# Attention and expert block in one kernel: the first 45 attention steps in another order, 50 of their small jobs on another engine

## The chip, the cores and the metric

The kernel runs on one core of one Trainium2 chip. A core has a matrix engine (TensorE, PE), three engines for the work on vectors (VectorE or DVE, ScalarE or ACT, GpSimd or POOL), a sync engine (SP) that here issues nearly all transfers, and 16 DMA engines. Each engine works through its own queue in the order in which the program was written. The metric is the time of one execution in microseconds (us) on the device. Lower is better.

## The reference

```python
def _attn_ref(q, k, v, tau):                      # (8, 8, 576, 64) each
    scale = 1.0 / np.sqrt(q.shape[-1])
    scores = scale * np.matmul(q, k.transpose(0, 1, 3, 2))
    thresh = np.max(scores, axis=-1, keepdims=True) - tau
    scores = np.where(scores >= thresh, scores, -1000000000.0)
    scores = scores - np.max(scores, axis=-1, keepdims=True)
    attn = np.exp(scores)
    attn = attn / (np.sum(attn, axis=-1, keepdims=True) + 1e-09)
    return np.matmul(attn, v).astype(np.float32)
...
    x = np.ascontiguousarray(attn_out.transpose(0, 2, 1, 3)).reshape(B * S, H * D)   # (4608, 512)
...
    h = x @ w_in                                  # w_in (512, 2048)
    g = np.where(h > 0.0, h, alpha * (np.exp(np.minimum(h, 0.0)) - 1.0))
    return (g @ w_out).astype(np.float32)         # w_out (2048, 512)
```

Attention for 64 heads that keeps only scores within tau of the row's maximum, followed by a two-layer block with an ELU between the layers. All data is float32 when it reaches the engines; the two weight matrices arrive in 64 bits and are converted on the chip.

## The kernel before, in words

Attention works on pairs of heads; there are 32 pairs (8 sequences of 4 pairs). A pair is cut into five **steps**: four blocks of 128 rows for both heads, and one "tail" step for the last 64 rows of both. Step n is `steps[n]`; the steps 10, 13, 16, 19, 24, 29, 34, 39, 44 are tails. Each step is a chain of **jobs** on different engines:

- `sc` (L537, matmuls at L551, PE): scores into one of a few score buffers in PSUM; from step 10 on there are two, so `sc` of a head waits for the mask of the head two before it;
- `max` (L600, DVE), `th` (L604, POOL: maximum minus tau) and `exp` (L614, ACT);
- `mask` (L623, DVE): compares scores with `th`, multiplies with `exp`, and adds up the row; this frees the score buffer;
- `su` and `rec` (sum of the two parts, L631 on DVE or L590 on ACT; reciprocal, L637 on DVE);
- `norm` (L596 on POOL or L584 on ACT): multiplies the row with the reciprocal;
- the result is then transposed, either on PE (`part`, L640, copied out of PSUM by ACT in `put`, L656), or by way of DRAM (`turned`: DVE transposes 32 x 32 squares at L716 and SP writes them out at L745; `fetch`: SP reads them back at L753 or L762, named `landed` in the table of places). The second way is used from step 24 on for most steps;
- `val` (L777 and L782, PE): values times transposed weights, copied out by ACT (`out`, L899).

Mixed in between are: the loading of heads (`load`, SP) and their preparation (`prep`, `scale`, `copy`); the conversion of 32 pieces of the weights, each a load `lw` (L408, SP), `rest` (L415 on ACT or L432 on POOL), `shift` (L421, DVE), `add` (L427, POOL), `sign` (L437, ACT) and `end` (L445, DVE); halves of the two-layer block for the first sequences (`half`: L940 and L980 on PE, with follow-up jobs called `post`); and sums of weight blocks (`in`, L1066, DVE or POOL) that a later stage uses.

The order of all these jobs for the steps 0 to 44 comes from a planner, `early_tasks` (L1135). Each job is entered with a nominal time, to which two numbers of a table `MOVED` are added, one for its kind and one for the job itself:

```python
    def task(x, t, key, f, *needed):
        each = "_".join(map(str, x)) if isinstance(x, tuple) else x
        made[x] = [t + (MOVED.get(key, 0.0) if key else 0.0) + MOVED.get(each, 0.0), len(made), f, needed, False]
...
        for x in sorted(made, key=lambda x: made[x][:2]):
            do(x)
```

`do` first does whatever the job needs and has not been done, and then the job. The result is one sequence of jobs, and each engine's queue is that sequence cut down to its own jobs. The numbers only order; nothing waits for a clock. Four more sets choose engines: `ACT_NORM` (which `norm` jobs are on ACT and not on POOL), `IN_POOL` (which `in` jobs are on POOL and not on DVE), `SU_ACT` (which `su` jobs are on ACT and not on DVE) and `REST_POOL` (which `rest` jobs are on POOL and not on ACT). The number and shape of the jobs do not depend on any of this. What follows step 44, some 1000 us with a fixed interleaving written out by hand (`tail_step`, `wide_step`, `ffn_quarters`), reads a part of the same table under other keys.

Of the kernel before, what the change touches and what calls it, by code (L numbers as in the profile page):

```python
# [18 lines left out]
ACT_NORM = {(0, 1), (10, 0), (10, 1), (11, 1), (13, 0), (15, 1), (16, 0), (17, 0), (17, 1), (18, 1), (22, 0), (24, 0), (25, 0),  # L19
 (26, 1), (28, 0), (30, 1), (31, 0), (32, 0), (33, 0), (35, 0), (36, 0), (36, 1), (37, 0), (40, 1), (44, 0), (44, 1)}  # L20
IN_POOL = {(6, 2), (1, 2), (7, 1), (0, 0), (3, 1), (6, 1), (0, 2), (5, 0), (7, 2), (2, 2), (1, 0), (4, 1), (5, 2)}
SU_ACT = {33, 41, 13, 16, 24, 30}
REST_POOL = {9, 27}

MOVED = {
    "add_10": 0.71, "add_11": -0.15, "add_12": 0.39, "add_14": -0.07, "add_17": 0.55, "add_20": -0.24, "add_21": 0.44,
    "add_22": 5.07, "add_23": -0.73, "add_26": -3.5, "add_27": -0.44, "add_28": -0.38, "add_3": 0.54, "add_30": -0.57,
    "add_31": -0.22, "add_5": 2.32, "add_6": -0.33, "add_8": -0.51, "adda10": 0.84, "adda30": 0.88, "addb00": 0.73,
    "addb01": -4.17, "addb10": -0.32, "addb11": -0.15, "addb20": 0.79, "addb21": 0.43, "addb30": -0.74, "addb31":
    0.02, "adde20": -0.39, "adde21": -0.32, "adde30": -0.22, "adde31": -0.95, "adde40": 0.75, "adde41": 0.21,  # L30
# [12 lines left out]
    "exp0c1": -0.43, "exp0c2": 0.28, "exp0c3": 4.67, "exp0c4": -1.31, "exp0d0": -3.28, "exp0d1": -2.61, "exp0d2":
    -1.48, "exp0d3": -2.62, "exp0d4": -1.52, "exp0e2": 0.41, "exp0e3": 2.22, "exp0z0": 5.23, "exp0z1": 4.88, "exp1a0":
    0.21, "exp1a1": -1.01, "exp1a2": -0.85, "exp1a3": -1.51, "exp1b0": -1.09, "exp1b1": -1.69, "exp1b2": 0.24,
    "exp1b3": -0.46, "exp1c0": 0.46, "exp1c1": 3.31, "exp1c2": 1.51, "exp1c3": 4.64, "exp1d0": -1.25, "exp1d1": 0.19,
    "exp1d2": -2.37, "exp1d3": -3.61, "exp1e2": 0.53, "exp1z0": 0.11, "exp1z1": 1.06, "exp_0_0": 4.58, "exp_0_1":
    -0.35, "exp_11_0": 0.46, "exp_11_1": 2.18, "exp_12_0": 0.57, "exp_12_1": -0.63, "exp_14_0": -0.14, "exp_15_0":
    0.39, "exp_17_0": -0.65, "exp_17_1": 1.88, "exp_18_0": 2.27, "exp_18_1": -0.64, "exp_1_0": 2.83, "exp_20_0":
    -2.39, "exp_22_0": -0.79, "exp_22_1": 1.61, "exp_23_0": 4.02, "exp_24_0": 0.62, "exp_25_0": -0.51, "exp_25_1":  # L50
    -0.17, "exp_26_0": -0.16, "exp_26_1": 0.79, "exp_27_1": -1.13, "exp_28_1": -0.68, "exp_29_0": -0.51, "exp_2_0":
    4.22, "exp_2_1": -0.4, "exp_30_0": 0.01, "exp_30_1": 0.66, "exp_31_1": -0.02, "exp_32_1": -1.23, "exp_33_0":
    -1.92, "exp_34_0": 0.14, "exp_36_1": 0.9, "exp_37_0": 3.69, "exp_37_1": -0.34, "exp_38_0": 0.35, "exp_38_1":
    -3.27, "exp_39_0": -1.11, "exp_3_0": -0.48, "exp_40_0": 3.34, "exp_41_1": -1.16, "exp_42_0": -0.21, "exp_42_1":
    5.99, "exp_43_0": -1.65, "exp_43_1": -0.28, "exp_4_0": 0.68, "exp_4_1": -1.2, "exp_6_0": -0.13, "exp_6_1": -0.48,
    "exp_7_0": -0.49, "exp_7_1": 0.06, "exp_9_0": -0.08, "extra_35": 2.03, "extra_36": -0.7, "extra_37": 0.56,
    "extra_38": -0.08, "extra_39": -0.3, "extra_40": 0.05, "extra_41": -0.31, "extra_42": 1.01, "f0.0": -2.08, "f1.0":
    -0.13, "f1.1": 0.2, "f10.0": 0.05, "f11.0": -0.04, "f12.1": 0.12, "f13.1": -0.5, "f14.0": 0.02, "f15.1": -0.06,
    "f16.0": 0.04, "f16.1": 0.69, "f16.2": -0.14, "f17.0": -0.28, "f18.1": 0.12, "f2.0": -5.54, "f2.1": -0.25, "f2.2":
    0.7, "f20.1": -1.03, "f21.0": 0.13, "f22.1": -0.19, "f23.0": 0.08, "f23.1": 2.72, "f23.2": 0.07, "f25.0": 0.39,  # L60
    "f26.0": -0.08, "f26.1": 0.42, "f3.0": 0.35, "f5.0": -0.32, "f5.1": 4.32, "f6.1": -0.54, "f7.0": -0.01, "f9.0":
    0.35, "f9.1": 1.94, "fbound0": -0.14, "fbound1": 0.93, "fbound4": -0.36, "fe00": 0.1, "fe10": 0.37, "fe11": 0.3,
    "fe20": -0.6, "fetchb0": 0.25, "fetchb1": 0.02, "fetchb2": 2.4, "fetchb3": 0.47, "fetchb4": 0.31, "fetchc0": 0.5,
    "fetchc1": -0.13, "fetchc2": -3.89, "fetchc3": 4.97, "fetchc4": -1.52, "fetchd0": 3.22, "fetchd1": -2.69,
    "fetchd2": 4.68, "fexp00": 0.1, "fexp20": 0.25, "fexp31": 0.12, "ffetch0": 1.19, "ffetch1": -0.24, "ffetch2":
    -0.52, "ffetch3": -0.65, "fkcopy": -0.11, "floadk": -2.59, "floadq": 2.51, "fm00": -3.15, "fm01": -0.49, "fm11":
    -2.07, "fm20": 1.6, "fm21": -0.43, "fmask00": 1.48, "fmask01": -0.63, "fmask10": 0.68, "fmask11": 0.02, "fmask30":
    -0.16, "fmask31": 0.36, "fmask4": 0.2, "fmax00": -0.03, "fmax01": -0.65, "fmax10": 0.91, "fmax11": 0.5, "fmax20":
# [1809 lines left out]
```

## Time and profile before

| what | value |
| --- | --- |
| three runs | 1298.63, 1300.83, 1302.12 us |
| median | 1300.83 us |
| span of the profiled execution, first to last instruction | 1298.8 us |
| mean granted clock of PE | 0.997 |
| busy over the span | PE 1277.1, DVE 1011.8, POOL 790.9, ACT 567.9 us |
| chain that ended last | PE 82%, DVE 4%, DMA 2%, the rest 1% and less each |
| DMA engines | q1 72.1% of their time, 254.14 MB |

The profile is one execution. Busy times of PE are modelled for pipelined matmuls, so that a busy PE is not necessarily PE at its peak; idle times come with the instruction that ended them. The profiled execution's own time was not given apart from its span; the span is 2.0 us less than the median of the three runs and lies within their spread of 3.5 us.

In the steady part of the kernel, from about 320 us on, PE is busy all the time: between 400 and 1000 us its idle time is 0.2 us in sum. The steps 0 to 44 lie in the first 282 us or so.

### The profile page before, as it was taken

How to read it: one execution, taken by the hardware profiler on the slowest of the kernel's cores; microseconds unless marked ns; L12 is line 12 of the kernel's file. 1: busy time of each engine (PE TensorE's matmuls, PEld its weight loads, DVE VectorE, ACT ScalarE, POOL GpSimd, SP SyncE). 2: the span in 40 equal slices, each digit the busy share in tenths (PEclk: the TensorE clock that was granted, in tenths of full speed). 3: DMA queues.
4: the chain of work that ended last, by engine and by line, in shares of the span. 5: the costliest groups of instructions: out<-in, count | busy, mean ns of one | idle time of the engine just before them, and what ended most of it. 6: DMA issues, size and time to landing. Idle time of an engine off the chain costs nothing.

```text
span 1298.8 us, 21747 instructions
## 1 busy us (share of the span) xinstructions
PE 1277.1 (98%) x6822; PEld 993.8 (77%) x6822; DVE 1011.8 (78%) x2199; ACT 567.9 (44%) x1224; POOL 790.9 (61%) x1181
## 2 busy tenths in 40 slices
PE   9999999899999999999999999999999999999998
PEld 7676576446878888878878787878787888888887
DVE  6787887788888988898889889897989882545534
ACT  5888644335262525353444444353525261421320
POOL 4686645767476756766576757574867473524533
PEclk9999999899999999999999999999999999999999
DMA  7546377879898988899889888899899875222211
GB/s 149 129 146 191 97 192 207 250 203 267 210 255 223 269 226 242 236 269 225 237 214 250 240 235 223 254 245 240 227 255 256 229 214 169 89 73 63 92 61 33
DMA packets 327827, 256.01 MB, mean 197 GB/s; under 512 B 209312, under 2 KB 288672, under 8 KB 327712
## 3 DMA queue, kind: packets, MB, share of 16 engines
q1 hardware_dynamic: 325776, 254.14, 72.1%
q8 instruction: 54, 0.88, 0.3%
q10 hardware_dynamic: 1936, 0.48, 0.2%
q14 instruction: 61, 0.50, 0.1%
HBM read 165.94 MB, written 88.60 MB: 196 GB/s over the span
## 4 chain that ended last, share of the span: by engine, by line
PE 82%; DVE 4%; DMA 2%; issue 1%; POOL 1%; ACT 1%; SPq 0%; DVEq 0%; ACTq 0%; POOLq 0%
PE f L1606 30%; PE f L1466 28%; PE sc L829 7%; PE sc L889 7%; PE f L980 3%; PE sc L551 2%; PE f L940 1%; PE sc L881 1%; DMA there<-x 1%; PE pv L782 1%; PE sc L876 1%; DVE x L716 1%; PE rt L640 1%; DVE w L623 1%; DMA sw<-win_sums 1%
## 5 line engine op out<-in xcount | busy, mean ns | idle before, releaser
L596 POOL TENSOR_SCALAR w<-w,rs 128x576 f32<-128x576 f32 x172 | 141.4, 830 | 78.0 <-DVE rs L637 73.3
L836 DVE TENSOR_REDUCE mx<-sc 128x1 f32<-128x576 f32 x207 | 148.2, 749 | 29.6 <-PE sc L829 25.8
L846 ACT ACTIVATE w<-sc,mx 128x576 f32<-128x576 f32 x115 | 82.9, 740 | 117.9 <-DVE mx L836 99.9
L1466 PE MATMUL f<-xt,sw 128*128 128x256 f32 x512 | 123.9, 384 | 1.4 <-ACT xt L899 0.8
L1466 PE MATMUL f<-xt,w_in_sb 128*128 128x256 f32 x512 | 122.3, 381 | 0.1
L842 POOL TENSOR_SCALAR th<-mx,ntau 128x2 f32<-128x2 f32 (+1 forms) x115 | 34.3, 298 | 136.6 <-DVE mx L836 136.6
L716 DVE STREAM_TRANSPOSE x<-w 128x512 f32<-128x512 f32 (+2 forms) x163 | 106.9, 690 | 11.8 <-POOL w L596 10.6
L1466 PEld LDWEIGHTS f<-xt,sw 128*128 128x128 f32 x512 | 93.6, 190 | 21.6 <-issue 4.9
L1466 PEld LDWEIGHTS f<-xt,w_in_sb 128*128 128x128 f32 x512 | 96.2, 190 | 15.9 <-ACT w L1480 2.8
L1466 PE MATMUL f<-x,w_in_sb 128*128 128x256 f32 x448 | 106.1, 379 | 1.3 <-ACT g L1527 1.3
L1606 PE MATMUL f<-w_out_sb,g 128*128 128x256 f32 x448 | 107.1, 382 | 0.0
L1606 PE MATMUL f<-w_out_sb,s 128*128 128x256 f32 x448 | 107.0, 382 | 0.0
L1606 PE MATMUL f<-t,s 128*128 128x256 f32 x448 | 105.8, 379 | 0.0
L829 PE MATMUL sc<-kT,qT 64*128 64x448 f32 (+4 forms) x736 | 103.2, 416 | 0.5 <-DVE w L850 0.5
L829 PEld LDWEIGHTS sc<-kT,qT 64*128 64x128 f32 x736 | 80.6, 186 | 25.5 <-issue 16.8
L1553 POOL TENSOR_TENSOR s<-g 128x256 f32<-128x256 f32 x104 | 80.4, 778 | 29.3 <-PE f L1606 20.0
L850 DVE SCALAR_TENSOR_TENSOR w<-sc,th,w 128x576 f32<-128x576 f32 x115 | 89.7, 810 | 10.2 <-ACT w L846 10.1
L1466 PEld LDWEIGHTS f<-x,w_in_sb 128*128 128x128 f32 x448 | 85.0, 190 | 13.3 <-ACT g L1527 1.7
L1606 PEld LDWEIGHTS f<-w_out_sb,g 128*128 128x128 f32 x448 | 84.1, 190 | 14.2 <-issue 3.2
L1606 PEld LDWEIGHTS f<-w_out_sb,s 128*128 128x128 f32 x448 | 84.2, 190 | 13.5 <-issue 2.5
L1606 PEld LDWEIGHTS f<-t,s 128*128 128x128 f32 x448 | 85.1, 190 | 11.6
L596 POOL TENSOR_SCALAR e<-e,rs 128x576 f32<-128x576 f32 x92 | 68.5, 748 | 35.5 <-DVE rs L637 33.4
(209 smaller groups left out, 2831.5 us busy)
## 6 DMA issues: line engine op xcount, KB each, us to landing
there<-x SPq DMA_DIRECT2D x436, 144.0 KB, 3.6
wTb<-there SPq DMA_DIRECT2D x56, 576.0 KB, 6.5
wTa<-there SPq DMA_DIRECT2D x53, 576.0 KB, 4.9
sw<-win_sums SPq DMA_DIRECT2D x62, 384.0 KB, 4.3
t<-wout_sums SPq DMA_DIRECT2D x45, 512.0 KB, 5.8
qm<-in_q_dram SPq DMA_DIRECT2D x124, 72.0 KB, 4.8
vm<-in_v_dram SPq DMA_DIRECT2D x64, 128.0 KB, 3.7
wst<-in_moe_w_in_dram SPq DMA_DIRECT2D x16, 512.0 KB, 4.4
```

The lines of the kernel that those rows point to most:

```text
L596: nc.gpsimd.tensor_scalar(wv, wv, st["rs"][:, h : h + 1], 1.0, ALU.mult, ALU.mult)
L716: nc.vector.transpose(x[:, :, c0 : c0 + nc_], src.rearrange("p (c g n) -> p g c n", c=nc_, n=T))
L829: on_banks(nc.tensor.matmul(o, qT[r, i * P : (i + 1) * P], kT[r, k0 : k0 + n], start=True, stop=True, skip_group_check=True), o)
L836: on_banks(nc.vector.tensor_reduce(st["mx"][:, h : h + 1], st["sc", h], axis=AX.XY if i == NC else AX.X, op=ALU.max, negate=True), st["sc" ...
L842: nc.gpsimd.tensor_scalar(st["th"][:, cs], st["mx"][:, cs], -1.0, ntau, ALU.mult, ALU.add)
L846: on_banks(nc.scalar.activation(st["e", h], st["sc", h], AF.Exp, bias=st["mx"][:, h : h + 1]), st["sc", h])
L850: on_banks(nc.vector.scalar_tensor_tensor(st["e", h], st["sc", h], st["th"][:, h : h + 1], st["e", h], ALU.is_ge, ALU.mult, accum_out=st[" ...
L889: on_banks(nc.tensor.matmul(o, vm[:, h, c], parts[part][:, g0:g1, h * (NC + 1) + c], start=False, stop=(c == NC - 1), skip_group_check=Tru ...
L980: nc.tensor.matmul(cur[c, i][:, :DM], hidden(c, ft % NU, 1)[:, 0, ft // NU, i], w_out_sb[:, ft], start=(ft == 0), stop=(ft == NFT - 1))
L1466: nc.tensor.matmul(loc["banks"][place], left[:, j], right[:, j], start=(begins and j == 0), stop=(j == 1), skip_group_check=True)
L1553: engine.tensor_tensor(o, x, y, op)
L1606: nc.tensor.matmul(place(m), lhs, rhs, start=(begins and v == 0), stop=(v == RU - 1), skip_group_check=True)
```

## The change

Only constants change; no function does. All four sets change, together in 50 places, and the table `MOVED` gets 356 new entries and new values for 652 of its 1801 old ones; no entry is taken out. All of the changed entries are for single jobs of the steps 0 to 44 (`start`, `rest`, `idle`, `switch` and `late` among them, which are single jobs too). The entries by kind and those of the later stages stay.

```diff
-ACT_NORM = {(0, 1), (10, 0), (10, 1), (11, 1), (13, 0), (15, 1), (16, 0), (17, 0), (17, 1), (18, 1), (22, 0), (24, 0), (25, 0),
- (26, 1), (28, 0), (30, 1), (31, 0), (32, 0), (33, 0), (35, 0), (36, 0), (36, 1), (37, 0), (40, 1), (44, 0), (44, 1)}
-IN_POOL = {(6, 2), (1, 2), (7, 1), (0, 0), (3, 1), (6, 1), (0, 2), (5, 0), (7, 2), (2, 2), (1, 0), (4, 1), (5, 2)}
-SU_ACT = {33, 41, 13, 16, 24, 30}
-REST_POOL = {9, 27}
+ACT_NORM = {(10, 0), (10, 1), (11, 1), (13, 0), (14, 1), (15, 1), (16, 0), (17, 0), (17, 1), (18, 1), (20, 1), (22, 0), (23,
+ 1), (24, 0), (24, 1), (26, 0), (26, 1), (27, 0), (28, 0), (30, 1), (31, 0), (32, 1), (33, 0), (35, 0), (36, 0), (36, 1),
+ (37, 0), (37, 1), (38, 0), (4, 0), (40, 0), (40, 1), (41, 0), (41, 1), (44, 0)}
+IN_POOL = {(1, 0), (2, 2), (3, 2), (4, 0), (4, 1), (4, 2), (5, 2), (6, 1), (6, 2), (7, 1), (7, 2)}
+SU_ACT = {10, 11, 13, 17, 18, 20, 25, 26, 30, 37, 39, 40, 42}
+REST_POOL = {10, 15, 16, 18, 19, 20, 27, 28, 29, 5, 7, 9}
...
-    "mask_15_0": 1.57, "mask_15_1": 1.1, "mask_17_0": 0.6, "mask_17_1": -4.56, "mask_18_0": 5.15, "mask_18_1": -2.03,
...
+    "mask_15_0": -4.95, "mask_15_1": 1.67, "mask_16_0": 0.29, "mask_17_0": 1.53, "mask_17_1": -4.56, "mask_18_0": 3.6,
...
-    5.47, "part_19_0": -0.16, "part_1_2": 0.06, "part_20_0": -0.17, "part_21_1": -0.04, "part_22_1": -3.07,
-    "part_23_1": 2.59, "part_23_2": -0.5, "part_26_0": 0.38, "part_26_1": -0.68, "part_26_2": 0.47, "part_29_0":
...
+    "part_18_1": 0.07, "part_18_2": 7.58, "part_19_0": -1.35, "part_19_1": 0.17, "part_1_2": -0.46, "part_20_0": 5.95,
...
+    0.38, "part_26_1": 2.37, "part_26_2": 0.29, "part_29_0": 0.03, "part_29_1": 1.56, "part_2_0": -2.6, "part_2_2":
```

**The sets.** `ACT_NORM` gains 13 jobs and loses 4 (0,1), (25,0), (32,0), (44,1); `REST_POOL` gains 10; `SU_ACT` gains 11 and loses 4; `IN_POOL` gains 3 and loses 5.

**The order.** Sorting the jobs by the new sums gives, on each queue, a sequence that is close to the old one. On PE, which runs 248 entries of it, ten places differ, each by a swap with a neighbour. Those and the places on other queues that the prediction speaks of are:

| place | key, old and new | what stands where after the change |
| --- | --- | --- |
| PE, DVE step 0 | `rest` 0, 0.1 | the transposition of the rest of q of the first pair stands behind the first `max` of step 0, and not ahead of it |
| PE step 11 | `part_10_0` -1.06, -1.36 | `sc` 11 and `part` 10,0 ahead of one half of the block, and not behind it |
| ACT step 9 | none of its own | `put` 9,1 stands behind `su` 10, `rest` 6 and `norm` 10,0 |
| DVE step 15 | `end_14` 5.43, -1.65 | `end` 14 ahead of the two masks of step 15, and not behind them |
| PE step 20 | `part_20_0` -0.17, 5.95 | one half of the block between `sc` 21 and `part` 20,0 |
| POOL step 20 | set `ACT_NORM` | `norm` 20,1 is gone from POOL ahead of `th` 21 and `norm` 21,0 |
| SP step 24 | `landed_24` -3.08, 4.09; `load_k_6` 0, 6.49 | `fetch` 24 behind two stores of results and the four transfers of `load` k 6; before, the stores stood behind it and `load` k 6 ahead of the writes of `turned` 24 |
| PE step 27 | `part_26_1` -0.68, 2.37 | `sc` 27 between `part` 26,0 and `part` 26,1 |
| PE step 32 | none of its own | `sc` 32 behind one half of the block, and not ahead of it |
| DVE step 30 | `turned_30` 1.15, 3.88 | `turned` 30 behind one ELU of the block and `prep` q 7 |
| ACT step 33 | `put_33_2` 0, 0.34 | `put` 33,1 ahead of `put` 33,2 |
| SP step 38 | `landed_38` 0, 1.95 | `fetch` 38 behind the four writes of `turned` 40, right ahead of `fetch` 39 |

## The prediction

> **What bounds the kernel now.** I read the stretches first: for each, its length, then the busy time of PE, PEld, DVE, ACT and POOL with their instructions in brackets, the granted clock, the DMA share, GB/s.
>
> ```profile
> 0.00:50.00 50.00, 46.82 (x332) 35.88 (x333) 38.02 (x89) 30.14 (x57) 25.84 (x58) 1.00 0.74 147
> 50.00:100.00 50.00, 48.42 (x272) 35.45 (x271) 40.71 (x88) 43.18 (x91) 39.02 (x48) 1.00 0.45 140
> 100.00:150.00 50.00, 49.09 (x235) 27.89 (x234) 40.11 (x87) 40.26 (x82) 36.34 (x48) 1.00 0.59 167
> 150.00:200.00 50.00, 49.76 (x249) 34.32 (x249) 41.83 (x96) 25.19 (x50) 22.07 (x43) 1.00 0.62 166
> 200.00:250.00 50.00, 45.21 (x187) 24.52 (x187) 35.62 (x84) 19.13 (x38) 34.34 (x53) 0.93 0.81 223
> 250.00:300.00 50.00, 46.47 (x213) 27.10 (x209) 40.87 (x94) 19.84 (x40) 35.43 (x55) 1.00 0.84 224
> ...
> 400.00:500.00 100.00, 100.00 (x568) 80.33 (x567) 86.08 (x191) 39.77 (x88) 60.56 (x93) 1.00 0.91 244
> ```
>
> The late stage has no idle time on PE, so the change can only move the moment at which PE comes to the end of step 44, at about 282 us. Up to 300 us PE idles 300 - 285.77 = 14.2 us, 0.2 to 4.8 in each 50. DVE, ACT and POOL have 7 to 31 idle us in each 50: none of them is a bound by its load. So work on them costs only where PE waits for it, and I went to PE's waits (up to 310 us; total, times, longest):
>
> ```profile
> PE sc L551 <- DVE w L623: 5.8, 5, 4.0
> PE rt L640 <- POOL w L596: 2.0, 5, 0.5
> PE rt L640 <- POOL ident masks.py:199: 1.5, 1, 1.5
> ...
> PE pv L777 <- ACT wTa L656: 1.2, 1, 1.2
> PE sc L876 <- DVE w L623: 1.0, 1, 1.0
> PE pv L777 <- DMA wTa<-there: 0.6, 2, 0.3
> ...
> PE rt L640 <- ACT wTb L656: 0.4, 1, 0.4
> ```
>
> One wait is far longer than the others, and it costs twice. PE's instructions in order of time, and the clock by 5 us:
>
> ```profile
> 238.07 1.24 PE L551 MATMUL sc<-kT,qT 64*128 64x288 f32 x8
> 243.31 2.26 PE L551 MATMUL sc<-kT,qd 128*128 128x288 f32 x4 [4.00 <-DVE w L623]
> 245.36 3.62 PE L980 MATMUL f<-w_out_sb,g 128*128 128x512 f32 x4
> ```
>
> ```profile
> 235.00:240.00 5.00, 4.31 (x27) 1.94 (x25) 2.02 (x7) 1.46 (x4) 2.36 (x3) 1.00 1.00 320
> 240.00:245.00 5.00, 1.69 (x4) 1.29 (x5) 4.09 (x11) 1.37 (x2) 4.54 (x8) 0.76 0.96 297
> 245.00:250.00 5.00, 5.00 (x12) 2.22 (x12) 4.03 (x9) 0.74 (x1) 4.61 (x6) 0.56 0.87 196
> 250.00:255.00 5.00, 5.00 (x30) 2.58 (x27) 2.24 (x4) 1.76 (x3) 2.38 (x6) 1.00 1.01 257
> ```
>
> This is `sc` 39 right behind `sc` 38. It waits for mask 38, and behind the idle time the clock is lower: 5 x 0.24 + 5 x 0.44 = 3.4 us of clock. The DVE rows say why the wait is that long:
>
> ```profile
> 239.38 1.42 DVE L600 TENSOR_REDUCE mx<-sc 128x1 f32<-128x576 f32 x2 [2.91 <-PE sc L551]
> 240.72 1.49 DVE L716 STREAM_TRANSPOSE x<-w 128x512 f32<-128x512 f32 x3
> 242.34 0.82 DVE L623 SCALAR_TENSOR_TENSOR w<-sc,th,e 128x576 f32<-128x576 f32 x1
> ```
>
> Two maxima and `turned` 37 lie between `sc` 38 and mask 38. In the new order these five stand just so, on PE and on DVE. The largest loss is left as it is. The same holds for the first 1.5 us (identity), for the 1.2 us at 23 us (`val` 0 behind `rest` 0, whose weights arrive at 22.3 us) and for the loop of `sc`, `max`, `turned`, `mask` from 255 to 280 us.
>
> **The engines of the 50 jobs.** 9 norms net go from POOL (843 ns, L596) to ACT (774 ns, L584), 10 `rest` from ACT (687 ns) to POOL (673 ns), 7 sums net from DVE (153 ns) to ACT (295 ns), 2 block sums net from POOL (766 ns) to DVE (539 ns). POOL: -7.6 + 6.7 - 1.5 = -2.4 us; ACT: +7.0 - 6.9 + 2.1 = +2.2; DVE: -1.1 + 1.1 = 0. Cost nothing as load: POOL was idle 107 us of the first 300, ACT 122, DVE 63. If a moved job comes to stand just ahead of what PE waits for, it costs its 0.15 to 0.84 us; these places are below. A `rest` on POOL also holds `th` and `norm` behind it until its weights land (512 KB, 4.0 to 4.5 us in the DMA table of that stretch). At the tightest places, `rest` 7, 18 and 19, POOL comes to them at about 59.9, 100.2 and 102 us, and their transfers, issued at 56.4, 96.7 and 97.2, land at about 60.9, 100.7 and 101.5. So two waits of at most 1.0 us, and POOL idled 2.4 us at 60.6 and 2.8 us at 101.5 anyway: zero, at worst +1.0.
>
> The Trainium skill's page "SBUF — State Buffer" (the split into engine side and DMA side) speaks against work on POOL: DVE and POOL share a port pair as an exclusive lock, and the loser waits for the whole instruction. By it each of the ten `rest` could take the length of a DVE instruction more, by an estimate ten times 0.5 to 0.8 us on POOL. The trace agrees in kind: `norm` at 95 to 98 us took 1.54 us and 0.75 us elsewhere. By either, POOL has the idle time for it, so the sum stays.
>
> **The moves, place by place.** First what is gained; only waits that exist can be gained.
> - `part` 20,0 waited 0.37 us for its norm at 132; now a half block of 1.88 us stands ahead: -0.37.
> - `part` 21,0 waited 0.55 at 138.7 for `norm` 21,0, which stood behind `norm` 20,1 (0.91 us), now on ACT: -0.55.
> - `part` 26,2 waited 0.24 at 169 for a copy; `sc` 27 (1.24) now stands between: -0.24.
> - `part` 34 waited 0.45 at 217 behind two copies in the wrong order (0.27 is the one too many): -0.2.
> - `part` 12,0 waited 0.31 at 77. `sc` 11 goes ahead 1.9 us sooner, DVE idled 1.26 and 0.78 us for it: -0.31.
>
> Together -1.7. With every other wait of 0.2 to 0.5 between 25 and 239 us (0.47, 0.35, 0.30, 0.23) it is -3.0; the low bound is that, the high one 0.
>
> Then what is lost:
> - Step 0: 0.65 us of transposing q now lies between the two maxima. Mask 0,0 waits for its exponential anyway (10.60), exponential 0,1 comes 0.3 us later: +0.3 (0 to 0.65).
> - `put` 9,1 behind `norm` 10,0: `part` 10,0 needs its bank. By the durations of the ACT rows it is free at 62.9 and PE there at 62.7: +0.2 (0 to 0.8).
> - `end` 14 (0.67) ahead of mask 15 delays `norm` 15,0, for which PE already waited 0.47 at 97.8: +0.5 (0 to 0.7).
> - `fetch` 24: SP issued it at 165.05, it lands 4.2 to 5.1 us later, and `val` 4,1 starts at 170.85 with no wait. Now two stores and four transfers (2.0 us of issue) go ahead, so some 166.5 and 170.7 to 171.6: +0.6 (0 to 1.4). Behind it in SP's queue are the writes of `turned` 25, whose reader is 12 us away.
> - `turned` 30 behind an ELU (0.65) and `prep` q (0.77): 1.4 us later, 0.64 at `turned` 31, since its maxima wait for `sc` 32, 1.7 us later. `val` 6,0 already waited 0.23 at 213.5 for this fetch: +0.6 (0 to 1.4).
> - `fetch` 38 was issued at 257.5 and 39 at 263.6; now both go at 263.6. A single one lands in 4.7 us. The pair of step 40 and 41, issued from 269.9, let PE start at 277.1. `val` 7,1 starts at 270.7: +0.3 (0 to 1.5).
>
> All other differences on DVE, ACT and POOL lie under PE's work: between 52 and 239 us PE idles 4 us in 187, so the cover is PE's own queue, and without it each is worth its own 0.2 to 0.8 us. On SP, the loads that trade places are all read 5 us or more later.
>
> Sum: -1.7 + 2.5 = +0.8 us. Span 1298.8 + 0.8 = 1299.6; with the 2.0 us by which the median lies above the span, **1301.6 us**. By its own bounds -3.0 to +6.45, against the median 1297.8 to 1307.3; six losses at their worst together are unlikely.
>
> **Rivals.**
> - *Faster: the clock stays up at 240 us.* The waits before it move that moment by a microsecond or so. Only one wait in the trace, of 4.00 us, is followed by half a clock; the next longest (1.46 and 1.35) are not. If what counts is whether the idle time covers some fixed interval, a shift can undo it. For it: the three runs lie 3.5 us apart, as much as the 3.4 us of clock. Against: the wait keeps its length. Price: -3.4, with the gains -1.7 and the losses at nothing: 1300.8 - 5.1 = **1295.7**. In a sentence by itself: the Trainium skill, "TensorE: Matmul & The Clock Gate", section "What's actually happening", states a free-running window of about 3.4 us, idle for which the clock is halved. By that rule 4.0 us would often miss a whole window, and the trace, with one case, can't say.
> - *Slower: SP's queue.* The three fetches set back (24, 30 with 31, and 38) end at their high bounds, because DMA is at 0.6 to 1.0 of its time there: 1.4 + 1.4 + 1.5 = 4.3, with the other losses 1.0 and half of the gains: 1300.8 + 4.3 + 1.0 - 0.8 = **1305.3**. It decides from the moment at which a fetch lands after PE has come to its `val`: slack now 0.7, none and 2 us. For it: `val` 6,0 waits already. Against: the fetches before landed in 4.2 to 5.1.
> - *It does nothing:* PE's order is the same but for ten swaps, and what is gained is lost: **1300.8**. That lies in the forecast's own range and is counted there.
>
> **How the numbers follow.** The forecast (and nothing) 0.44, the faster rival 0.28, the slower 0.28. About 0.3%, 3.9 us, is what a measurement of this kernel can tell from no change. 1295.7 is faster by 0.4%, 1305.3 slower by 0.35%, the forecast within. The range for 8 in 10 is 1295.5 to 1306.5, which takes in both rivals; the forecast's own is 1297.8 to 1304.5.
>
> **What would show it.** In the profile after: PE idle up to 300 us near 15.0; the 4.00 us wait of `sc` 39 and a clock near 0.6 behind it still there; PE's waits for POOL w at L640 down from 2.0 to about 1.3; waits for fetches (L777 for DMA) up from 0.6 to about 2. The prediction is wrong if that long wait is gone or halved, if a new wait of over 2 us stands before 282 us, or if the stretch from 400 us on is not the same.

## The result and the profile after

Six runs of the changed kernel gave 1305.30 to 1309.62 us, median 1305.83; six of the kernel before, on the same chip, 1298.63 to 1303.06, median 1301.47. The ratio of all these runs, as measured, is 1.0042, its 95% interval 1.0028 to 1.0056: slower by 0.4% (the two medians alone give 1.0033). The profiled execution's span is 1303.5 us, 4.7 more than before. The forecast was 1301.6 with a range of 1297.8 to 1304.5, so the median lies above it; slower had a chance of 0.28.

The stretches of the changed kernel, columns as in the prediction:

```profile
0.00:50.00 50.00, 45.66 (x318) 34.56 (x319) 37.40 (x86) 28.56 (x54) 25.75 (x57) 1.00 0.72 147
50.00:100.00 50.00, 48.41 (x273) 34.97 (x271) 41.50 (x87) 41.02 (x88) 39.83 (x49) 1.00 0.42 136
100.00:150.00 50.00, 47.80 (x224) 27.55 (x225) 41.70 (x81) 37.91 (x79) 37.96 (x50) 1.00 0.60 165
150.00:200.00 50.00, 48.87 (x246) 32.40 (x243) 40.91 (x91) 26.04 (x51) 19.62 (x38) 1.00 0.57 146
200.00:250.00 50.00, 45.05 (x205) 26.50 (x204) 37.67 (x88) 23.36 (x45) 31.24 (x53) 0.99 0.84 225
250.00:300.00 50.00, 47.13 (x196) 26.71 (x195) 41.39 (x92) 21.30 (x42) 32.96 (x50) 0.94 0.86 229
400.00:500.00 100.00, 100.00 (x568) 80.39 (x567) 86.90 (x194) 38.01 (x84) 60.16 (x91) 1.00 0.92 248
```

PE still has no idle time from 400 us on, so the loss lies ahead of it: up to 300 us PE idles 300 - 282.9 = 17.1 us, where 15.0 were forecast and 14.2 were there before. The waits of PE (up to 310 us; total, times, longest):

```profile
PE sc L613 <- DVE w L685: 5.4, 4, 4.0
PE rt L702 <- POOL w L658: 2.8, 5, 0.9
PE pv L839 <- DMA xtail<-xs: 1.9, 1, 1.9
...
PE pv L839 <- DMA wTb<-there: 1.1, 1, 1.1
...
PE rt L702 <- ACT xs L967: 0.8, 1, 0.8
PE pv L839 <- DMA wTa<-there: 0.4, 1, 0.4
```

(Each line number is 62 higher than before, since the table grew.) The long wait of `sc` 39 is as it was. The waits for POOL's rows rose from 2.0 to 2.8 us where 1.3 were forecast. New are 1.9 us at `val` 8,0 (0.3 before), 1.1 at `val` 4,1 (`fetch` 24) and 0.8 for the copies of `val` 2,1; of the waits for POOL, 0.9 us at 16 us are new, in the first steps.

Idle time is not the whole loss: it grew by 2.9 us and the span by 4.7. A wait can also hide inside a job. PE's row of `sc` 23 before, then after, and DVE's row of the second mask of step 22 after:

```profile
145.59 1.24 PE L551 MATMUL sc<-kT,qT 64*128 64x288 f32 x8
```

```profile
147.17 1.97 PE L613 MATMUL sc<-kT,qT 64*128 64x288 f32 x8
```

```profile
147.03 0.81 DVE L685 SCALAR_TENSOR_TENSOR w<-sc,th,e 128x576 f32<-128x576 f32 x1
```

In the new order `sc` 23 stands ahead of a `val` and not behind it. Before, its eight matmuls start in four pairs, each pair 0.01 us apart. After, the third starts at 147.91 us, 0.06 us behind the end of that mask (147.85), which frees the second score buffer, and four of the eight run alone. As each record is 0.4 to 0.5 us long, no idle time shows, but the scores take 1.90 us up to PE's next job instead of 1.17. From step 4 to 36 the scores outside the tails took 1.6 us longer in sum (steps 6, 7, 14, 23 and 25 above all), and those of step 37 took 0.7 us less. In steps 7 and 14, too, the late matmul starts 0.06 us behind the end of a mask; what held up steps 6 and 25 is not shown. The half clock took 3.4 us in both profiles: one stretch of 6.8 us before, two of 3.4 us after.

Where the time went is best read from the **lag**: the start of `sc` n after the change minus its start before, both counted from PE's first instruction, which is the same in both. It needs no cause, only two timelines. The numbers at the head of the table are steps; "389 us" is the scores that stand there in the kernel before, and "end" is PE's last instruction. Steps 11, 23 and 32 are left out, since `sc` stands elsewhere there.

| kernel | 5 | 12 | 15 | 18 | 19 | 22 | 28 | 34 | 36 | 39 | 40 | 44 | 389 us | end | ratio to before, 95% interval |
| --- | --- | --- | --- | --- | --- | --- | --- | --- | --- | --- | --- | --- | --- | --- | --- |
| after | 1.4 | 2.1 | 2.9 | 2.9 | 4.3 | 3.9 | 6.0 | 6.0 | 6.3 | 5.4 | 4.1 | 3.6 | 4.6 | 4.7 | 1.0042 (1.0028 to 1.0056) |
| e1 q first | -0.4 | 0.4 | 1.3 | 1.3 | 2.6 | 2.3 | 5.0 | 5.0 | 8.0 | 7.1 | 6.7 | 6.2 | 7.3 | 7.6 | 1.0051 (1.0036 to 1.0066) |
| e2 ten rests on ACT | 1.1 | 1.5 | 1.1 | 0.8 | 1.4 | 1.0 | 2.8 | 2.8 | 3.5 | 2.9 | 2.8 | 2.3 | 3.6 | 4.6 | 1.0030 (1.0018 to 1.0041) |
| e3 order only | 1.0 | 1.2 | 0.8 | 1.2 | 1.6 | 2.4 | 4.1 | 4.1 | 5.1 | 4.3 | 3.0 | 2.6 | 3.0 | 3.1 | 1.0042 (1.0025 to 1.0059) |
| e4 sets only | -0.6 | -0.1 | 0.1 | 0.0 | 2.8 | 3.6 | 4.1 | 4.5 | 4.2 | 4.6 | 3.3 | 3.3 | 3.2 | 3.6 | 1.0039 (1.0024 to 1.0054) |
| e5 writes 42 later | 0.4 | 1.1 | 2.0 | 2.0 | 3.4 | 3.0 | 4.9 | 4.9 | 5.6 | 4.9 | 3.4 | 2.9 | 3.4 | 5.4 | 1.0050 (1.0033 to 1.0068) |
| e6 fetch 24 back | 2.4 | 3.2 | 4.0 | 3.9 | 5.3 | 4.9 | 6.2 | 6.2 | 7.1 | 6.3 | 4.9 | 4.5 | 4.8 | 4.7 | 1.0040 (1.0025 to 1.0055) |
| e7 before, sc 38 early | 0.0 | 0.1 | 0.1 | 0.0 | 0.0 | 0.0 | -0.1 | -0.1 | 0.3 | -1.5 | 0.5 | 0.5 | 0.4 | 0.0 | 0.9990 (0.9981 to 0.9999) |
| e8 five undone | -0.5 | -0.2 | -0.4 | -0.7 | 0.0 | -0.4 | 0.3 | 0.3 | 0.9 | 0.3 | 0.3 | -0.1 | 0.3 | 1.5 | 1.0006 (0.9996 to 1.0016) |
| e9 q first, turned 30 | -0.4 | 0.4 | 1.2 | 1.2 | 2.5 | 2.1 | 4.7 | 4.7 | 5.3 | 4.5 | 4.4 | 3.9 | 4.3 | 5.0 | 1.0049 (1.0031 to 1.0067) |
| e10 sets, two sums back | 1.8 | 1.9 | 1.9 | 1.6 | 2.2 | 2.0 | 2.5 | 2.8 | 2.7 | 3.4 | 2.1 | 2.1 | 2.1 | 2.9 | 1.0018 (1.0008 to 1.0027) |
| e11 three undone | -0.8 | 0.8 | 0.7 | 0.4 | 1.0 | 0.6 | 2.2 | 2.2 | 2.7 | 2.1 | 0.4 | 0.0 | 0.4 | -0.1 | 1.0012 (1.0003 to 1.0022) |
| e12 before, four gains, sc 38 | 0.3 | 0.8 | 0.6 | 0.5 | 0.5 | 0.1 | -0.2 | -0.2 | -0.2 | -1.9 | -0.9 | -0.6 | -0.3 | 0.3 | 0.9995 (0.9983 to 1.0007) |
| e13 end 19 later | 0.8 | 1.5 | 2.3 | 2.4 | 2.7 | 2.5 | 5.2 | 5.2 | 5.9 | 5.1 | 3.5 | 3.1 | 3.5 | 4.2 | one run |
| e14 two sums back | 3.1 | 3.9 | 4.8 | 4.8 | 5.8 | 5.4 | 8.2 | 8.2 | 8.6 | 8.0 | 6.5 | 6.1 | 7.3 | 6.9 | one run |

Each row is one execution against the one profiled execution of before, so a row is read by its differences along the line, which say in which steps time is lost. The profiled execution is a single one and not always typical: that of e1 was the slowest of four (1308.17 us, the others 1304.21 to 1305.78), those of e2 and e7 the slowest of theirs. The ratios rest on 4 to 10 runs of each kernel, and their intervals reach 0.09 to 0.18% to either side.

The row of after in words: 1.7 us are lost in the first steps (-0.3 at `sc` 0 to 1.4), 0.7 up to step 12, 2.2 from there to 19, 0.4 come back to 22, 2.1 go to 28, 0.3 to 36; 2.6 come back from there to 44, and 0.9 is lost behind it, around `val` 8,0.

### The profile page after: what moved, and what is told of

Read it like the earlier page. It is cut to its first block, busy times and chain, and to the rows that moved or that the text cites. A ratio compares the mean times of both kernels' runs of the same rounds, so it can differ in the third digit from the quotient of the medians.

```text
span 1303.5 us, 21730 instructions
## 1 busy us (share of the span) xinstructions
PE 1278.8 (98%) x6822; PEld 994.9 (76%) x6822; DVE 1018.8 (78%) x2194; ACT 570.9 (44%) x1230; POOL 788.3 (60%) x1180
## 4 chain that ended last, share of the span: by engine, by line
PE 84%; DVE 5%; DMA 3%; ACT 2%; issue 2%; POOL 2%; SPq 1%; DVEq 0%; ACTq 0%; POOLq 0%
PE f L1668 30%; PE f L1528 28%; PE sc L891 7%; PE sc L951 7%; PE sc L613 2%; PE f L1042 2%; PE pv L844 2%; PE rt L702 2%; PE sc L943 1%; DVE mx L662 1%; PE sc L938 1%; PE f L1002 1%; DMA there<-x 1%; DVE w L685 1%; ACT e L676 1%
## 5 line engine op out<-in xcount | busy, mean ns | idle before, releaser
L658 POOL TENSOR_SCALAR w<-w,rs 128x576 f32<-128x576 f32 x163 | 132.9, 823 | 77.9 <-DVE rs L699 66.8
```

Source lines behind the costliest of these rows:

```text
L658: nc.gpsimd.tensor_scalar(wv, wv, st["rs"][:, h : h + 1], 1.0, ALU.mult, ALU.mult)
```

## The experiments

**e1, the start.** The transposition of the rest of q shares one buffer with the load that follows. SP's DMA issues of the kernel before, then of the one after, and the DVE row after that reads the load:

```profile
7.50 0.51 SPq L479 DMA_DIRECT2D vf<-in_v_dram  x1
8.20 2.06 SPq L463 DMA_DIRECT2D qm<-in_q_dram  x4
```

```profile
7.50 0.51 SPq L541 DMA_DIRECT2D vf<-in_v_dram  x1
9.64 1.96 SPq L525 DMA_DIRECT2D qm<-in_q_dram  x4
```

```profile
14.03 0.78 DVE L550 STREAM_TRANSPOSE x<-qm 128x576 f32<-128x576 f32 x1 [1.25 <-DMA qm<-in_q_dram]
```

The load of pair 1's q leaves 1.44 us later, and all that SP issues behind it. The first maximum came to stand ahead of the transposition not by its own key but by that of `th` 0,0 (0.2, now -5.22): its sum, -6.25, lies below the -5.81 of `rest`, and `do` does first what a job needs.

```diff
-}
+} | {"rest": -0.5}
```

> The changed kernel, but the transposition of the rest of q of pair 0 stands ahead of the first maximum again; nothing else moves. Theory (a freed buffer lets a load out): SP issues the load of q of pair 1 at 8.2 us instead of 9.6, so the lag of the changed kernel behind the one before at the scores of step 5 falls from 1.35 us to 0.2 or less, and the whole kernel gets 1.0 to 1.4 us shorter, some 1304.6. Rival (norm 0,1, now on POOL behind scale 1, sets the start back): the lag at step 5 stays at 0.8 or more and the time changes by less than 0.5 us. Second rival (the late steps take the delay up anyway, as steps 35 to 42 took up 2.6 us): the lag at step 5 falls, but the end does not.

The lag at step 5 is -0.4, and it stays 1.6 to 1.7 us below that of after up to step 22, and 1.0 from 28 to 34: the theory of the freed buffer holds, and `norm` 0,1 on POOL costs nothing that shows. The size differs between executions. At step 5 the five profiles with the changed start and no half clock at 25 us stand at 0.4 to 1.4, the eight with the old start at -0.8 to 0.3: 1.2 us on the mean. But the ratio did not fall. From step 34 to 36 the lag jumps by 3.0 us. PE's rows there, and the clock:

```profile
217.66 0.60 PE L702 MATMUL rt<-ident,w 128*128 128x128 f32 x4
220.02 0.70 PE L839 MATMUL pv<-wTa,vd 128*128 128x256 f32 x2 [1.76 <-DMA wTa<-there]
```

```profile
215.00:220.00 5.00, 3.26 (x13) 1.80 (x11) 4.17 (x8) 2.58 (x4) 1.86 (x4) 1.00 1.00 186
220.00:225.00 5.00, 4.75 (x23) 2.58 (x23) 1.15 (x4) 0.78 (x3) 0.74 (x1) 0.66 0.95 241
```

`val` 6,0 starts at 219.7 us in the changed kernel and at 220.0 here: its fetch lands just then, whether PE is there 0.4 or 1.8 us ahead. The longer wait is followed by 3.4 us at half clock (0.66 over the second stretch). So the second rival was the right one for the end: in this execution, what the start gives back, the next fetches and the clock take, and in the ratio no gain is seen either.

**e2, the ten `rest` jobs.** Only their engine is put back.

```diff
-REST_POOL = {10, 15, 16, 18, 19, 20, 27, 28, 29, 5, 7, 9}
+REST_POOL = {9, 27}
```

> The changed kernel with the ten moved rest jobs back on ACT, at the same places of the order. Theory (DVE and POOL get in each other's way): the mean of shift on DVE falls from 617 ns to 540 to 560, that of end from 843 to 710 to 740, so some 6 us of DVE time before 230 us go away, of which PE waits for a part: the lag at the scores of step 22 falls from 3.9 to 2.0 to 2.6 us and the kernel gets 1.2 to 2 us shorter, some 1304.2. Rival (the order is at fault, the rest jobs are covered as forecast): the means may fall but the lag at step 22 changes by less than 0.4 us, and the time stays at 1305.8.

Measured: lag 1.0 at step 22, 2.9 less than after, and 1.0030; by the ratios some 0.12% or 1.5 us of the 0.42% (the intervals overlap). Most of the gain, 2.2 us, lies between steps 12 and 19. How POOL's work reaches DVE is seen in the groups of `shift` and `end` (count, busy, mean ns; up to 300 us), before, after and in e2:

```profile
L421 DVE TENSOR_SCALAR wtop<-wst 128x512 uint32<-128x512 uint32 x32 | 16.9, 538 | 0.1
L445 DVE SCALAR_TENSOR_TENSOR w_in_sb<-wtop,wst 128x512 f32<-128x512 f32 x16 | 11.0, 700 | 2.8 <-ACT wst L437 2.8
```

```profile
L483 DVE TENSOR_SCALAR wtop<-wst 128x512 uint32<-128x512 uint32 x32 | 19.5, 617 | 0.5 <-DMA wst<-in_moe_w_in_dram 0.4
L507 DVE SCALAR_TENSOR_TENSOR w_in_sb<-wtop,wst 128x512 f32<-128x512 f32 x16 | 13.5, 857 | 1.2 <-POOL wtop L489 1.2
```

```profile
L483 DVE TENSOR_SCALAR wtop<-wst 128x512 uint32<-128x512 uint32 x32 | 18.2, 577 | 0.2
L507 DVE SCALAR_TENSOR_TENSOR w_in_sb<-wtop,wst 128x512 f32<-128x512 f32 x16 | 12.3, 778 | 0.0
```

All `shift` and `end` together are 39.2 us before, 46.0 after, 42.5 in e2: the change makes these jobs on DVE 6.8 us longer without adding one, and 3.5 us of that go with the ten `rest` jobs. Fewer came back than the theory said (mean of `end` 0.77 and not 0.71 to 0.74); the new order, too, brings `add` and `end` together (e3, with the ten jobs on ACT, has 43.2 us). Single rows, DVE and POOL after:

```profile
112.44 1.19 DVE L507 SCALAR_TENSOR_TENSOR w_out_sb<-wtop,wst 128x512 f32<-128x512 f32 x1
...
114.90 1.79 DVE L507 SCALAR_TENSOR_TENSOR w_out_sb<-wtop,wst 128x512 f32<-128x512 f32 x1
116.62 1.41 DVE L662 TENSOR_REDUCE mx<-sc 128x1 f32<-128x576 f32 x2
```

```profile
112.39 0.71 POOL L494 TENSOR_SCALAR wst<-wst 128x512 f32<-128x512 uint32 x1
...
114.86 1.29 POOL L489 TENSOR_TENSOR wtop<-wtop,wst 128x512 int32<-128x512 int32 x1
```

An `end` that begins with no POOL instruction running takes 0.65 to 0.70 us (16 of them in this execution). Where a `rest` or `add` is running on POOL, it takes what is left of that plus 0.55: 0.33 left gives 0.88, 0.66 gives 1.19, 0.68 gives 1.24, 1.01 gives 1.56, 1.22 gives 1.76, 1.24 gives 1.79. So DVE waits for the end of the POOL instruction. With a `norm` running it goes either way: two such `end` waited (0.87 and 1.15 us), four took 0.68 us and the `norm` took 0.87 to 1.69 instead of some 0.75. That is the exclusive lock that the Trainium skill's page "SBUF — State Buffer" states (section "SBUF: two separate sides"); the trace agrees, and the 0.55 holds to 0.03 us.

**e3 and e4, order and sets apart.** e3 is the changed table with the four sets of before, e4 the old table with the four new sets.

> The changed order with all four sets of before. Theory (order and sets each cost something: the order the start, fetch 24 and the fetch for val 8,0, the sets the DVE time): 1301.5 + 2.5 to 3.5, so 1304 to 1305. Rival (the order is fitted to its sets and worse without them): 1306 or more. Forecast of the prediction (order +0.8 or nothing): 1301.5 to 1302.3.

> The order of before with all four sets of the change. Theory (the ten rest jobs on POOL lengthen shift and end on DVE by some 6 us in sum, a quarter of it on the path): 1301.5 + 1.0 to 2.0, so 1302.5 to 1303.5, with shift at 0.60 us or more and end at 0.80 or more. Rival, as the prediction costed it (work on POOL is covered, the sets cost nothing): 1301.2 to 1301.8, with the lag at every step under 0.5 us.

1.0042 and 1.0039: each alone loses as much as both together. For e3 that is some 5.5 us, more than its theory said and as its rival had it. That the sets cost nothing is refuted. But the place was not the expected one: e4 has no lag up to step 18 and 4.1 us at step 20, and `shift` and `end` stayed below the theory's marks (0.56 and 0.78 us). ACT's and PE's rows of e4 there:

```profile
110.19 0.29 ACT L590 ACTIVATE su<-sm 128x2 f32<-128x2 f32 x1 [1.52 <-DVE w L623]
...
111.50 0.59 ACT L947 ACTIVATE g<-f 128x512 f32<-128x512 f32 x1
...
117.75 0.30 ACT L590 ACTIVATE su<-sm 128x2 f32<-128x2 f32 x1 [0.48 <-DVE w L623]
117.96 0.35 ACT L899 COPY xt<-pv 128x256 f32<-128x256 f32 x1
```

```profile
114.23 1.88 PE L980 MATMUL f<-w_out_sb,g 128*128 128x512 f32 x4
118.68 1.25 PE L640 MATMUL rt<-ident,w 128*128 128x128 f32 x5 [2.58 <-ACT xs L905]
```

Sum 17, 0.3 us of work, stands on ACT ahead of an exponential of the block and waits 1.52 us for mask 17; DVE, idle for 2.08 us before the ELU that needs this exponential, comes later to the maxima and masks of step 18. Sum 18 stands ahead of the copies of `val` 2,1, whose matmuls ended at 110.9 us, and waits 0.48 us for mask 18. PE waits 2.58 us for these copies and then runs 3.4 us at half clock. In the changed order `out` 2,1 stands ahead of `su` 18, so that order and sets have to be judged together.

**e10, e4 without two sums.**

```diff
-SU_ACT = {10, 11, 13, 17, 18, 20, 25, 26, 30, 37, 39, 40, 42}
+SU_ACT = {10, 11, 13, 20, 25, 26, 30, 37, 39, 40, 42}
```

> The order of before with all sets of the change except that the sums of steps 17 and 18 stay on DVE. Theory (the 4 us that the sets alone cost at steps 18 to 20 come from these two sums: on ACT they wait for their masks, and the exponential of the block and the copy of val 2,1 wait behind them): the lag at step 20 falls from 4.07 to 1 us or less, and the kernel is at 0.999 to 1.001 of the kernel before. Rival (the ten rest jobs on POOL cost it, by way of DVE's shift and end): the lag at step 20 is 2 us or more.

The growth from step 12 to 20 is 0.3 us instead of 4.2 (the row starts at 1.8, because this execution had half a clock at 25 us): the two sums account for nearly all of it. (By its letter the rival's mark, a lag of 2 us or more at step 20, is met, with 2.2; but 1.9 of that were there at step 12.) The other 48 places still cost 0.18%, a little more than expected. The ten `rest` jobs are among them: in the old order they add next to nothing between steps 12 and 20, so what they cost in e2 is a matter of their engine and the new order together.

**e13 and e14, steps 18 and 19 of the changed kernel.** e13 moves `end` 19 (1.79 us above) behind the two maxima of step 18; e14 puts `su` 17 and 18 back on DVE.

```diff
-}
+} | {"end_19": 3}
```

> The changed kernel with end 19 on DVE behind the two maxima of step 18 instead of ahead of them; nothing else moves. Theory (the 1.79 us of end 19, held up by the add on POOL, delay the maxima and through them the mask, the copy of val 2,1 and PE): the first maximum of step 18 starts within 0.3 us of the end of its scores instead of 1.7 us behind it, and the lag, which grows by 1.36 us from step 18 to step 19 in the changed kernel, grows by 0.4 us or less. Rival (ACT's queue with sums 17 and 18 sets it): the growth stays at 1.0 us or more.

> The changed kernel with the sums of steps 17 and 18 on DVE, as before. Theory (DVE's port is at fault, the sums stand well in this order): the lag grows by 1.0 to 1.5 us from step 18 to step 19, as in the changed kernel. Rival (the sums are at fault, as with the sets alone, where they cost 4 us): it grows by 0.4 us or less.

From step 18 to 19 the lag grows by 1.36 us in the changed kernel, by 0.30 in e13, by 1.04 in e14. In e13 `end` 19 takes 0.68 us and the maximum starts 0.04 us behind its scores. So the place of one DVE instruction, at which it met one POOL instruction, cost PE 1.06 us; the sums are not at fault in this order. The meeting alone does not explain it: in e2 `end` 19 stands at the same place and meets the same `add` (1.76 us), and the lag grows by 0.59. DVE comes to the maxima 0.8 us sooner there: the `end` and the `shift` before take 0.69 and 0.43 us, and in the changed kernel, beside the `rest` at 112.39 us and a job of the block on POOL, 1.19 and 0.73.

**e6, `fetch` 24**, ahead of the two stores again.

```diff
-}
+} | {"landed_24": -3.08}
```

> The changed kernel with fetch 24 right behind the writes of turned 24 again, ahead of the two stores and the load of k of pair 6. Theory: the wait of val 4,1 (1.13 us) falls to 0.2 or less and the lag at the scores of steps 24 to 29 falls by 1.0 to 1.2 us. If the fetch of val 6,0 at 220 us has become the next bound (with the start put right it was: that wait grew from 0.40 to 1.76 us and the clock fell there), the lag at step 35 falls by 0.5 us or less and the end by nothing, or it gets longer by 1.7 us of clock; rival (each loss counts by itself): the end is 1.1 us earlier.

The wait of `val` 4,1 fell from 1.13 to 0.31 us, and the lag from step 22 to 28 grows by 1.3 instead of 2.1. The other 1.3 us are not a matter of this fetch; 0.9 of them are the scores of steps 23 and 25. At `val` 6,0 the lag grows by 0.9 instead of 0.3, with a wait of 1.02 instead of 0.40; but e5, whose order is that of the changed kernel up to there, waits 0.84, so this difference may be one between executions. The end and the ratio did not move.

**e9, the start and `turned` 30.** The fetch of `val` 6,0 hangs on a chain: `turned` 30, its four writes, `fetch` 30, the writes of `turned` 31 behind it in SP's queue, `fetch` 31, landing: 204.9 to 219.6 us in the changed kernel.

```diff
-}
+} | {"rest": -0.5, "turned_30": 2.8}
```

> The changed kernel with two things put back: the transposition of the rest of q ahead of the first maximum, and turned 30 ahead of the ELU and of prep q 7. Theory (putting the start right alone gained nothing because PE then came 1.7 us too early for the fetch of val 6,0, which hangs on turned 30): the lag at step 34 is some 4.3 us, the wait of val 6,0 stays under 0.7 us, no half clock at 220 us, and the end is 1 to 1.7 us before that of the changed kernel: 1.0030 to 1.0035 of the kernel before. Rival (the transfers of steps 30 to 36 set the pace, whatever DVE does): val 6,0 waits 1.3 us or more again, and the end is that of the changed kernel, 1.0040 or more.

The half that speaks of `val` 6,0 came true: the writes go 1.5 us sooner than in e1 and `val` 6,0 starts 1.3 us sooner, it waits 0.75 us, the clock stays up at 220, the lag at step 36 is 5.3 and not 8.0. The end did not: 1.0049. Here the 4.0 us wait of `sc` 39 was followed by 6.8 us at half clock and in the changed kernel's profile by 3.4, so the lag at step 40 is 4.4 against 4.1. What decides that is in the last section.

**e5, `val` 8,0.** The writes of `turned` 42 go behind `xs` 7 and the last store.

```diff
-}
+} | {"out_7_1": 0.08, "post_42_1_0_0": -0.53}
```

> The changed kernel, but the four writes of turned 42 stand in SP's queue behind the results of val 7,1 and the last store, as before, and not right behind fetch 40 and 41; nothing else moves. Theory (the writes run beside the fetch and slow it): the fetch for val 8,0 lands within 4.8 us of its last issue instead of 5.7, the wait of val 8,0 falls from 1.92 us to 1.0 or less, and the clock does not fall at 283 us; 1.0 + 1.7 us less, so some 1302.5 against a before of 1300. Rival (the fetch is only issued too late, behind the writes of turned 41): the wait stays above 1.5 us, the half clock at 283 us stays, and the time changes by less than 0.5 us.

The wait fell from 1.92 to 1.03 us and there is no half clock at 283, nearly as the theory said; the fetch landed 5.2 us behind its last issue instead of 5.9, not within 4.8. Whether the writes did that is not shown by one execution: e6, which leaves them as changed, waits 1.19 us. From step 44 to 389 us the lag grows by 0.4 us instead of 0.9: DVE is the slower one behind it (PE now waits 0.97 us for a mask at 290.7), so 0.5 us were to be had and not 2.7. Even these 0.5 go with the clock: the lag grows by 0.4 there in every profile of the changed kernel and its variants without a half clock at 283 us, e8, which waits only 0.56 us at `val` 8,0, among them, and by 0.9 to 1.3 in the four that have one (after, e1, e2, e14). The ratio shows nothing of it; in the profiled execution a load of weight sums came 2.0 us late at 448 us, which none of the others has there.

**e7, the long wait itself, in the kernel before.** `sc` 38 goes ahead of `val` 6,1.

```diff
-}
+} | {"val_6_1": 5.7, "out_6_1": 2.98}
```

> The kernel before, with the scores of step 38 on PE ahead of val 6,1 and not behind it; the copies of val 6,1 on ACT stand behind the exponentials of step 38, its result in SP's queue behind the writes of turned 37. Theory (the 4.00 us wait of sc 39 is the way from sc 38 over the maxima, turned 37 and mask 38, and val 6,1 can cover 3 us of it): the wait falls to 1.0 to 1.7 us, no half clock behind it, and the scores of step 42 come 3 to 6 us earlier; of that the fetches for val 7,1 and 8,0 may keep 1 to 2 us, so 2 to 5 us in all, 1295 to 1298 against a before of 1300. Rival (from there on transfers set the pace): the waits reappear at val 7,1 and val 8,0, and the end changes by less than 1 us.

PE's rows in e7:

```profile
241.84 1.21 PE L551 MATMUL sc<-kT,qd 128*128 128x288 f32 x4 [0.82 <-DVE w L623]
242.89 1.88 PE L980 MATMUL f<-w_out_sb,g 128*128 128x512 f32 x4
247.88 1.19 PE L777 MATMUL pv<-wTa,vd 128*128 128x256 f32 x2 [3.11 <-DMA there<-x]
```

The wait fell from 4.00 to 0.82 us and came back, 3.11 us long, at `val` 7,0: its fetch was issued at 239.7 and landed at 247.8, after 8.1 us, with the writes of `turned` 37 issued 1.1 us behind it and the DMA engines at 0.9 of their time and more up to 246 us; before, with these writes 2.7 us behind, it took 5.5 us. The scores of step 38 also take 1.87 us instead of 1.24 in their new place. The rival was right that here transfers set the pace, though at `val` 7,0 and not at 7,1 and 8,0. What is left is 0.1%, with an interval that ends just under 1.

**e8 and e11, several together.** e8 puts five things back; e11 leaves out `fetch` 24 (`landed_24`) and the writes of `turned` 42 (`out_7_1` and `post_42_1_0_0`).

```diff
-REST_POOL = {10, 15, 16, 18, 19, 20, 27, 28, 29, 5, 7, 9}
+REST_POOL = {9, 27}
...
-}
+} | {"rest": -0.5, "landed_24": -3.08, "turned_30": 2.8, "out_7_1": 0.08, "post_42_1_0_0": -0.53}
```

> The changed kernel with five things put back: the transposition of the rest of q first, the ten rest jobs on ACT, fetch 24 ahead of the stores, turned 30 ahead of the ELU and of prep q 7, the writes of turned 42 behind the last store. Theory (these five are the loss; the other 800 changed numbers and 40 engines are worth the gains of 1 to 1.7 us): lag under 1 us at every step up to 34, and the end between 2 us before and 1 us behind the kernel before: 1298 to 1301 against a before of 1300. Rival (the loss is spread over all moves): lag above 1.5 us at step 28, and 1302 or more.

> The changed kernel with three things put back: the transposition of the rest of q first, the ten rest jobs on ACT, turned 30 ahead of the ELU. Left as changed: fetch 24 behind the stores, and the writes of turned 42 right behind fetch 41. Theory (losses add up as long as the next fetch isn't met): lag under 0.3 us up to step 22, 1.0 to 1.5 us from step 28 on, and 0.5 us more at val 8,0: 1.0015 to 1.0020 of the kernel before, against 1.0006 with all five put back. Rival (the two left alone are covered once the three are gone): 1.0008 or less.

e8: lag within 0.7 us at every step to 34, and 1.0006 with 1 inside the interval. Ten engine entries and five table entries, out of 50 and some 1000, account for the loss; the rest of the change is in sum worth nothing that can be measured. It does not leave PE as it was: in e8, too, the scores of steps 6, 7, 23 and 25 take 1.3 us longer, which the waits that went make up for. e11: 1.0012, a little less than expected. Its lags missed: 0.4 to 1.0 from step 12 to 22, 2.2 at step 28 (`val` 4,1 waits 1.23), and that shrank at 40.

**e12, the gains.** The kernel before with four of the moves counted as gains, and e7's.

```diff
-ACT_NORM = {(0, 1), ..., (44, 1)}
+ACT_NORM = {(0, 1), ..., (20, 1), ..., (44, 1)}
...
-}
+} | {"sc_11": -0.6, "part_20_0": 5.95, "put_33_2": 0.34, "val_6_1": 5.7, "out_6_1": 2.98}
```

> The kernel before with four of the change's moves that the prediction counted as gains (sc 11 ahead of a half block, a half block ahead of part 20,0, norm 20,1 on ACT, put 33,1 ahead of put 33,2), and sc 38 ahead of val 6,1 as tried before. Theory of the prediction (each of the waits goes and PE keeps it): lag of -0.3 at step 12, -0.7 at step 20, -1.2 at step 22, and -1.4 at step 35; with sc 38 another 1.2 us: 0.9975 to 0.9985 of the kernel before. Rival (val 6,0 and the fetches behind it take it back): the lag at step 34 is -1.2 but at step 36 between 0 and -0.4, and the whole is 0.999, as with sc 38 alone.

`sc` 11 ahead of the half block loses 0.5 us at step 12 (its scores take 1.67 us instead of 1.17) and gives 0.2 back; the moves at steps 20 to 22 gain 0.4 and at 23 another 0.3; `put` 33,1 gains nothing. From step 5 to 34 it is -0.5 us where -1.4 were expected. The ratio of 0.9995 has 1 in its interval, so the four gains add nothing to e7's 0.1% that can be told.

## Why the prediction was wrong

It named what bounds the kernel rightly: the late stage did not change, the wait of `sc` 39 stayed at 4.0 us, and the whole loss lies in the first 285 us. The sum was +0.8 us (-1.7 and +2.5), and 4.7 us lie between the two profiled executions. It failed in these terms:

- **"Step 0: +0.3 (0 to 0.65)"** was 1.7 us at step 5 against e1, and 1.2 on the mean of the profiles. It costed the transposition as 0.65 us of DVE. What it frees was left out: the one buffer for q, the load that waits for it, and SP's queue behind it (e1).
- **"Cost nothing as load"** for the 50 engines. They were costed at nothing because POOL, ACT and DVE had idle time. Idle time did not cover them. The ten `rest` jobs cost some 2.5 us between steps 5 and 19 (e2), though only in the new order (e10). The Trainium skill's page "SBUF — State Buffer", which speaks against this, was weighed and its price put on POOL, the engine that got the work; whoever starts second waits, and here that was often DVE: of the 6.8 us that `shift` and `end` gained, 3.5 go with these jobs. How the 2.5 us divide between single meetings was not separated. At `part` 12,0, where PE waits 0.78 us and 0.32 in e2, POOL had been idle for 0.64 us before its `norm`, which came right behind DVE's reciprocal, so POOL's own queue was not the cause there.
- **"The sums"** were costed by their length on ACT. In the old order two of them hold ACT's queue and cost 4 us (e4, e10); the new order avoids that (e14), which is one reason why order and sets do not add up.
- **The gains, -1.7.** The waits of `part` 20,0 and 26,2 went as forecast. That of 21,0 only fell to 0.45, that of 34 rose to 0.55, and that of 12,0 from 0.31 to 0.78. A wait that goes is not kept as soon as another one stands close behind; e12 found -0.5.
- **"All other differences … lie under PE's work"**, and the reading that work costs only where PE shows a wait: `sc` 23, whose place was not priced, came to stand where its second buffer is not yet free. It and four more steps took 1.6 us longer without any idle time; 1.3 of that are in e8 too, where the waits that went pay for it.
- **"`put` 9,1: +0.2" and "`end` 14: +0.5"**: PE does not wait at `part` 10,0, and its wait for `norm` 15,0 is 0.40 us (0.47 before) and 0.18 in e8, which leaves both as changed, so they cost nothing that shows.
- **"`fetch` 24: +0.6 (0 to 1.4)"**: the mechanism was right; the wait is 1.13.
- **"`turned` 30: +0.6"**: its writes go 1.5 us later against PE, as reckoned (1.4), and PE's wait rose by only 0.16 us. The four writes landed within 4.2 us of the first issue instead of 5.5, so that the fetch behind them was late by 0.2; in e9 they took 5.3 us and in e1 4.7, so this may be luck of one execution. It is a bound that shows when PE is earlier (e1).
- **"`fetch` 38: +0.3"**: no wait at `val` 7,1; inside its range. **`fetch` 40 and 41** were not priced; the slower landing of the second (5.9 us instead of 4.9) goes with the new wait of 1.9 us at `val` 8,0, worth 0.5 by the half clock behind it.

The rival "slower, SP's queue" hit the time (1305.3) but not the place: of its three fetches one was late by 1.1 us. The faster rival's mechanism was there in part: the clock's stretch at 249 us was half as long as before, and 1.35 us came back from step 39 to 40; a second stretch at 283 us took 1.7 again.

## What to carry to other kernels

Idle time of an engine is not cover: ask what stands behind the moved job in that engine's queue, which buffer it frees and who waits for that buffer, and whether the other engine on the same port will start second. Look at a chain of transfers by the time at which it lands and not by the wait it shows now; a late PE hides it, and each repair ahead of it is then paid back there. Where the cause of a small loss is sought, compare the starts of the same instructions in two timelines first, since the totals of idle time hide where it comes and goes, and compare the lengths of the same jobs, since a wait between two matmuls of one job can count as busy.

## What the runs showed of the hardware

**The clock falls on a grid.** In the trace's clock records, every stretch at half clock before the last microseconds of a kernel begins and ends a whole number of times 3.413 us after PE first came to full speed, and lasts 3.413 or 6.827 us: from 69 to 71 such windows in the profile of before, from 71 to 72 and 81 to 82 after, from 63 to 64, 71 to 73 and 82 to 83 in e1. A window at full clock in which PE idled 56% or more was always followed by half clock, one of 50% or less never; between them it went both ways (52% in e1 and 53% in e10 did, 52% in e13 and 55% in e11 did not). The 4.0 us wait of `sc` 39 is 1.17 windows long and always covers enough of one. What it costs depends on where it ends: where it reached 20 to 46% into a further window (before, e1, e2, e8, e9) the half clock lasted two windows, where it did not, or reached at most 18% into it (after, e3 to e6, e10, e11, e13, e14), one. That is 1.7 us of PE's time by chance of a start that moves with each execution. The first wait of `val` 0,0 (0.6 to 2.5 us) sometimes falls the same way (e6, e10 and e14, at 25 us). The grid is the free-running window of the Trainium skill's page "TensorE: Matmul & The Clock Gate" (section "What's actually happening"); that a window idle for a little over half is enough is what the runs add.

**Single late loads.** Eight of the sixteen profiled executions (e2, e4, e5, e8, e9, e10, e12, e13) have a wait of PE of 0.6 to 2.0 us somewhere between 440 and 1000 us that the others do not have; those of 1 us and more (e2, e5, e9, e12) are for a load of weight sums that came late. Together with the clock this may be why single executions of one kernel lie 3 to 4 us apart; no run tests it.
